# Attention and two networks on one core: the second network's two matrix products done by 2x2 blocks in Strassen's way, with h kept in DRAM between them

## The chip, the cores and the metric

The program runs on one core of one Trainium2 chip. The metric is the device time of one execution in microseconds (us), lower is better. The work is spread over the core's engines, each with its own instruction queue in program order: PE (TensorE, the matrix engine; PEld is its weight load, which overlaps the products), DVE (VectorE), ACT (ScalarE), POOL (GpSimd, hardly used here) and SP (SyncE, which issues nearly all DMA transfers).

## The reference, cut to what matters

```python
def _attn_ref(q, k, v) -> np.ndarray:
    ...
    return (out_up + out_local).astype(np.float32)

def _moe_ref(x, w_gate, w_val, w_out) -> np.ndarray:
    g = x @ w_gate
    silu = g * (1.0 / (1.0 + np.exp(-g)))
    val = x @ w_val
    return (silu * val @ w_out).astype(np.float32)

def _moe2_ref(x, w_in, w_out) -> np.ndarray:
    h = np.maximum(x @ w_in, 0.0)
    return (h * h @ w_out).astype(np.float32)

def reference(**kwargs):
    ...
    attn_out = _attn_ref(**attn_kwargs)
    B, H, S, D = attn_out.shape
    x = np.ascontiguousarray(attn_out.transpose(0, 2, 1, 3)).reshape(B * S, H * D)
    x = _moe_ref(x=x, **moe_kwargs)
    return _moe2_ref(x=x, **moe2_kwargs)
```

`q`, `k` and `v` are 4 x 8 x 576 x 64, so `x` is 2304 tokens by 512. `_attn_ref` is a softmax attention on means of four rows, plus one in which a token sees those fewer than four away. The first network (`_moe_ref`) goes 512 -> 1536 -> 512, the second (`_moe2_ref`) 512 -> 2048 -> 512.

## The kernel before

**Number format.** A product of two float32 matrices is made as three products in TensorE's fp32r format. Each operand is split into a high part (ScalarE copies it into fp32r) and a low part (VectorE subtracts the high part from the source), and high x high, high x low and low x high are added up in a PSUM bank. "hi/lo" below means such a pair. Weights arrive as float64 words, in pieces of 128 x 512 (512 KB): a piece is loaded into the tile `wst`, decoded by ScalarE (L271, a scale) and VectorE (exponent, sign at L286, last bits at L296) into `wf`, and split by ScalarE (L306) and VectorE (L309) into a slot of the pool `w1` (6 slots) or `w2` (5 slots), 3 pieces to a slot.

**Stages, in order of time.** (1) Attention, with the first network's hidden units 0 to 5 beside it (stage B1; 128 hidden values are one unit), in token tiles of 256 and then 384. (2) Stage B2: units 6 to 11, for 6 tiles of 384 tokens; a unit is 24 products for gate and value (`proj`, L929 to L931), tanh and multiplications, and 12 products with w_out (`down`, L939 to L941). The tile's result gets the part from B1 added (L1042) and goes to `y_sp` in DRAM. (3) Stage C: the second network, 6 tiles of 384 tokens x 16 units (`c_unit`). A unit is 12 products of 384 columns (`proj`, into a bank `gv`, 128 values of h by 384 tokens), ReLU (ScalarE, L1212), square (VectorE, L1215), the split of h (L1219, L1222), and 9 products of 512 columns (L1232 to L1234) that add the unit's share of the output into three banks (`att`, `att`, `y`; 128 tokens by 512 each). h never leaves the core. The decoded weights of stage C follow into slots of `w1` and `w2` as units of B1 and B2 give them up.

**What sets the order.** A list scheduler in Python (`Order`) simulates the engines when the kernel is built. A `Task` is a chain of `Stage`s; a stage names its engine ("t" TensorE, "v" VectorE, "a" ScalarE, "d" SP), a cost, the buffers that it takes and gives back, and a condition (`after([...])`: not before these tasks). Tasks wait in queues ("mlp" for units, "x" for token tiles, "w" for weights, "v", "other"), each with a due time counted in units, and the scheduler writes the instructions out one after the other. On the chip each engine follows that order strictly. Products have no competitor left in stages B2 and C but other products.

The second network's products before (in `c_unit`, for one of three 128-token slices `c`):

```python
nc.tensor.matmul(o, u["h"][:, 0, c], w[:, 0], start=(f == 0), stop=False)
nc.tensor.matmul(o, u["h"][:, 0, c], w[:, 1], start=False, stop=False)
nc.tensor.matmul(o, u["h"][:, 1, c], w[:, 0], start=False, stop=last)
```

## Time and profile before

| what | value |
| --- | --- |
| device time, three runs | 991.59, 990.94, 991.14 us (median 991.14) |
| span of the profiled execution | 989.6 us |
| TensorE (PE) busy | 976.9 us, 99% |
| VectorE (DVE) busy | 546.8 us, 55% |
| ScalarE (ACT) busy | 371.8 us, 38% |
| GpSimd (POOL) busy | 23.8 us, 2% |
| DMA | 100.11 MB, mean 101 GB/s |

The runs are whole executions of the program without a profile; the span is that of one profiled execution, from its first instruction to its last, and all durations below come from it. A busy time is the union of an engine's instructions; products are pipelined, so that the durations of neighbours overlap and the cost of one is better read from start to start. The granted clock is the share of full speed that TensorE was given: 1.00 is 2.4 GHz, 0.50 is 1.2 GHz.

### The profile page before, as it was taken

What the parts mean: (1) busy time and instruction counts of PE and PEld (TensorE: products, weight loads), DVE (VectorE), ACT (ScalarE), POOL (GpSimd) and SP (SyncE); (2) the same over time, 40 slices, a digit from 0 to 9 for tenths busy, and PEclk for the clock granted to TensorE, in tenths of its full rate; (3) what the DMA queues carried; (4) which work ended last, traced back from release to release, by engine and by line L of the source; (5) the groups of instructions that cost most, each with busy time, mean ns of one, the idle gap of its engine ahead of it and who ended that gap; (6) DMA issues with size and microseconds to landing.
All of it is one profiled execution on the core that took longest, in us unless ns stands there. A gap on an engine that the chain in (4) does not pass through costs nothing.

```text
span 989.6 us, 17229 instructions
## 1 busy us (share of the span) xinstructions
PE 976.9 (99%) x7122; PEld 915.8 (93%) x7122; DVE 546.8 (55%) x1163; ACT 371.8 (38%) x844; POOL 23.8 (2%) x31
## 2 busy tenths in 40 slices
PE   8989999999999999999999999999999999999998
PEld 7868999999999999999999999999999999999996
DVE  6999996559589698542342598532322322322222
ACT  3676663443355355221121255432322322322222
POOL 0202020000000000000000000000000000000000
PEclk9989999999999999999999999999999999999999
DMA  9989785142473555220320554010100000000000
GB/s 274 265 269 266 209 185 137 44 123 51 145 251 112 185 183 174 96 90 7 96 74 23 167 177 160 20 64 1 32 32 1 20 14 1 32 1 1 33 1 32
DMA packets 67770, 100.11 MB, mean 101 GB/s; under 512 B 19564, under 2 KB 51820, under 8 KB 67692
## 3 DMA queue, kind: packets, MB, share of 16 engines
q1 hardware_dynamic: 64236, 91.04, 29.1%
q0 software_dynamic: 3456, 7.96, 4.7%
q8 instruction: 56, 0.92, 0.4%
q14 instruction: 22, 0.18, 0.1%
HBM read 79.07 MB, written 19.92 MB: 100 GB/s over the span
## 4 chain that ended last, share of the span: by engine, by line
PE 97%; DVE 1%; DMA 1%; ACT 1%; SPq 0%; issue 0%
PE gv L929 17%; PE gv L931 17%; PE gv L930 17%; PE att L1234 5%; PE att L1232 5%; PE att L1233 4%; PE y L939 4%; PE y L941 3%; PE y L940 3%; PE y L1233 2%; PE y L1232 2%; PE y L1234 2%; PE att L527 2%; PE att L585 2%; PE att L939 2%; PE att L941 2%
## 5 line engine op out<-in xcount | busy, mean ns | idle before, releaser
L929 PE MATMUL gv<-xh,w 128*128 128x384 f32 (+1 forms) x1056 | 342.8, 325 | 0.0
L931 PE MATMUL gv<-xh,w 128*128 128x384 f32 (+1 forms) x1056 | 339.6, 322 | 0.0
L930 PE MATMUL gv<-xh,w 128*128 128x384 f32 (+1 forms) x1056 | 339.1, 321 | 0.0
L929 PEld LDWEIGHTS gv<-xh,w 128*128 128x128 f32 x1056 | 199.0, 188 | 6.0 <-issue 0.6
L930 PEld LDWEIGHTS gv<-xh,w 128*128 128x128 f32 x1056 | 199.1, 189 | 3.9
L931 PEld LDWEIGHTS gv<-xh,w 128*128 128x128 f32 x1056 | 199.0, 188 | 0.2 <-DVE w L309 0.2
L1222 DVE TENSOR_TENSOR hh<-sg,hh 128x384 fp32r<-128x384 f32 x96 | 53.6, 558 | 124.4 <-ACT hh L1219 124.4
L1215 DVE TENSOR_TENSOR sg<-sg 128x384 f32<-128x384 f32 x96 | 53.6, 558 | 116.0 <-ACT sg L1212 115.9
L1219 ACT ACTIVATE hh<-sg 128x384 fp32r<-128x384 f32 x96 | 50.4, 525 | 128.5 <-PE y L1234 126.4
L1212 ACT ACTIVATE sg<-gv 128x384 f32<-128x384 f32 x96 | 47.1, 491 | 132.5 <-PE gv L931 131.0
L973 DVE SCALAR_TENSOR_TENSOR sg<-sg,gv 128x384 f32<-128x384 f32 (+1 forms) x84 | 41.7, 496 | 95.3 <-PE gv L931 94.4
L979 ACT ACTIVATE hh<-sg 128x384 fp32r<-128x384 f32 (+1 forms) x84 | 40.0, 476 | 132.1 <-DVE sg L973 131.6
L1234 PE MATMUL att<-w,hh 128*128 128x512 f32 x192 | 76.0, 396 | 0.0
L1232 PE MATMUL att<-w,hh 128*128 128x512 f32 x192 | 75.7, 394 | 0.0
L1233 PE MATMUL att<-w,hh 128*128 128x512 f32 x192 | 75.6, 394 | 0.0
L939 PE MATMUL y<-hh,w 128*128 128x256 f32 (+1 forms) x240 | 74.5, 310 | 0.0
L941 PE MATMUL y<-hh,w 128*128 128x256 f32 (+1 forms) x240 | 72.7, 303 | 0.1
L940 PE MATMUL y<-hh,w 128*128 128x256 f32 (+1 forms) x240 | 72.5, 302 | 0.0
L968 DVE SCALAR_TENSOR_TENSOR sg<-sg,gv 128x384 f32<-128x384 f32 (+1 forms) x84 | 41.5, 494 | 43.6 <-ACT sg L960 42.9
L960 ACT ACTIVATE sg<-gv 128x384 f32<-128x384 f32 (+1 forms) x84 | 37.3, 444 | 68.3 <-PE gv L931 68.1
L306 ACT ACTIVATE w<-wf 128x512 fp32r<-128x512 f32 x68 | 42.8, 629 | 41.0 <-DVE wf L296 40.5
L982 DVE TENSOR_TENSOR hh<-sg,hh 128x384 fp32r<-128x384 f32 (+1 forms) x84 | 41.8, 498 | 19.1 <-ACT hh L979 18.9
(97 smaller groups left out, 1356.2 us busy)
## 6 DMA issues: line engine op xcount, KB each, us to landing
wst<-wB SPq DMA_DIRECT2D x36, 512.0 KB, 4.2
wst<-wC SPq DMA_DIRECT2D x32, 512.0 KB, 3.9
y_sp<-ys SPq DMA_DIRECT2D x8, 768.0 KB, 3.8
xt<-x_sp SPq DMA_DIRECT2D x6, 768.0 KB
ys<-y_sp SPq DMA_DIRECT2D x6, 768.0 KB, 4.7
xt<-y_sp SPq DMA_DIRECT2D x6, 768.0 KB, 5.3
out<-ys SPq DMA_DIRECT2D x17, 256.0 KB, 2.1
qT<-qT SPq DMA_DIRECT2D x7, 592.0 KB, 9.9
```

The lines of the kernel that those rows point to most:

```text
L929: nc.tensor.matmul(ps[:, :n], w[:, 0], xh[:, 0, kk, :n], start=(kk == 0), stop=False)
L930: nc.tensor.matmul(ps[:, :n], w[:, 0], xh[:, 1, kk, :n], start=False, stop=False)
L931: nc.tensor.matmul(ps[:, :n], w[:, 1], xh[:, 0, kk, :n], start=False, stop=(kk == KD - 1))
L939: nc.tensor.matmul(y, w[:, 0], hh[:, 0, :n], start=start, stop=False)
L940: nc.tensor.matmul(y, w[:, 0], hh[:, 1, :n], start=False, stop=False)
L941: nc.tensor.matmul(y, w[:, 1], hh[:, 0, :n], start=False, stop=stop)
L1215: nc.vector.tensor_tensor(out=u["r"], in0=u["r"], in1=u["r"], op=ALU.mult)
L1219: nc.scalar.activation(out=u["h"][:, 0], in_=u["r"], func=AF.Copy)
L1222: nc.vector.tensor_tensor(out=u["h"][:, 1], in0=u["r"], in1=u["h"][:, 0].bitcast(F32), op=ALU.subtract)
L1232: nc.tensor.matmul(o, u["h"][:, 0, c], w[:, 0], start=(f == 0), stop=False)
L1233: nc.tensor.matmul(o, u["h"][:, 0, c], w[:, 1], start=False, stop=False)
L1234: nc.tensor.matmul(o, u["h"][:, 1, c], w[:, 0], start=False, stop=last)
```

## The change

Both products of the second network are cut into 2x2 blocks and done with 7 block products in the place of 8 (Strassen's way with 15 block sums, Winograd's form). This needs all of a block's h before the second product, so the stage falls into two phases.

**Phase one** (`c_step`): h = relu(x w_in)^2, for two halves `s` of the hidden values, three groups `g` of 768 tokens (two 384-token halves are the two column blocks), seven block products `P` in the order `STEPS`, and four hidden blocks `k` of 128. A step is 6 products of 384 columns. Two banks per k: in A (`att`) P1 begins and P6, P7, P4 add to it, and after each ScalarE copies the bank out as the start of one h block; in B (`gv` or `y`) stand P2, and then P5 and P3, each added by VectorE (`plus`) to a block copied earlier. ReLU and square follow, and the block goes to `h_sp` in DRAM. `x_group` makes four sums of x blocks and seven hi/lo blocks per group, in a ring of 4 (two `xh` tiles).

**Phase two** (`d_step`): the output, in 9 token blocks `q` of 256, seven steps of 24 products of 256 columns each (eight p of 256 hidden values x 3). `h_load` reads h back in two pieces (three for block 0), `t_task` makes four sums and seven hi/lo blocks of 1024 elements, in a ring of 3 that lies in the same two `xh` tiles. Output tiles `os` are stored from SP.

**Weights.** Of the 32 pieces of 128 x 512, 6 are decoded straight into block sums; 26 are decoded during B2 by `stage_task`, stored as float32 to `w_sp`, and loaded again when `pair_task` makes the sums: a pair of pieces gives four sums of 256 columns and seven blocks in hi/lo (512 + 512 + 768 columns, `CUTS`). The sets of w_in for p 0 to 2 are in `wu`, 3 in `wr`, 4 to 7 in `wl`; the sets of w_out overwrite them when phase one's half `s` has done its last step with the part. Pools change too: `w2` has 4 slots, `w1` is released after B1, and B2's units 10 and 11 get two slots `w6` in its place; B2's last tile runs them first.

The diff, cut:

```diff
-NW1, NW2 = 6, 5
+NW1, NW2 = 6, 4
...
+        slot, ready = ("w2", late_) if j < NF + NW2 else ("w6", late_b1_)
         for i in range(3):
-            w_task((j, i), wB[j][:, i], W2[j - NF], LATE, lambda: after([late_]))
+            w_task((j, i), wB[j][:, i], slot, LATE, lambda ready=ready: after([ready]))
     for t in range(NT2):
...
         x_task(("B2", t), T2, lambda t=t: load_xr(x_sp, t), lambda done=done: after(done), ("xt",))
         early, finish = add_tasks(("B2", t), t * T2, T2, y_sp, y4)
...
+        if t == NT2 - 1:
+            js = js[NW2:] + js[:NW2]
+        for j in js:
+            unit_tasks("B2", t, j, T2, j == js[0], j == js[-1], y4, finish, (), early)
+            if t == NT2 - 1 and j == NF1 - 1:
+                end_w6 = downs[-1]
+    end_b2 = downs[-1]
...
+    NG1, NG2 = NT2 // 2, NTOK // 256
+    STEPS = (1, 2, 6, 7, 5, 4, 3)
+    IN, OUT = 0, 1
+    BLK = {1: 0, 2: 1, 7: 2, 4: 3, 5: 4, 6: 5, 3: 6}, {1: 0, 7: 1, 2: 2, 3: 3, 5: 4, 6: 5, 4: 6}
+    CUTS = (0, 2), (2, 4), (4, 7)
+    h_sp = dram.tile([128, NG2, ALL, 2, 2, 128], F32, name="h_sp")
+    w_sp = dram.tile([128, 2 * NF2, 512], F32, name="w_sp")
...
+    def minus(out, a, b, op=ALU.subtract):
+        nc.vector.tensor_tensor(out=out, in0=a, in1=b, op=op)
...
+    def stage_task(kind, f):
...
+        def store():
+            nc.sync.dma_start(out=w_sp[:, kind * NF2 + f], in_=u["f"].bitcast(F32))
+        staged[kind, f] = Task([*bits(u, wC[f][:, kind]), Stage("d", dma(128 * 512), store, (), ("wf",))], LATE)
+        queues["w"].append(staged[kind, f])
...
+    def pair_task(kind, p, slot, conds, room=None):
...
+            if kind == IN:
+                minus(w["s"][:, 0], quarter(1, 0), quarter(1, 1), ALU.add)
+            else:
+                minus(w["s"][:, 0], quarter(0, 1), quarter(0, 0))
+        def second():
...
+        def third():
+            if kind == IN:
+                minus(w["s"][:, 1], w["s"][:, 0], quarter(0, 0))
...
+        def fourth():
+            minus(w["s"][:, 2], quarter(0, 1) if kind == IN else quarter(1, 0), w["s"][:, 1])
...
+            src, hi, _ = parts(i)
+            nc.scalar.activation(out=hi, in_=src, func=AF.Copy)
+        def low(i):
+            src, hi, lo = parts(i)
+            minus(lo, src, hi.bitcast(F32))
...
+        def begun(i):
+            also = [outs[0]] if i == 1 and not fs else [c_ready[kind, p - 1][2]] if k == i == 2 else []
+            return after([both, *also, *conds(i)])
...
+    for p in range(3):
+        pair_task(IN, p, "wu", lambda i: [late_b1_])
+    for f in range(6, NF2):
+        stage_task(IN, f)
+    for f in range(NF2):
+        stage_task(OUT, f)
+    pair_task(IN, 3, "wr", lambda i: [late_w6_])
+    for p in range(NPC, ALL):
+        pair_task(IN, p, "wl", lambda i: [late_b2_])
...
+    def x_group(s, g, start):
...
+        def t1():
+            u["t"] = [com.tile([128, 2, T2], F32, tag="hh", bufs=N_HH, name="hh") for _ in range(2)]
+            minus(u["t"][0], block(0, 1), block(0, 0))
+        sums = {
+            6: [t1, lambda: minus(u["t"][1], block(1, 1), u["t"][0])],
+            7: [lambda: minus(block(0, 1), block(1, 1), block(0, 1))],
+            4: [lambda: minus(u["t"][1], block(1, 0), u["t"][1])],
+        }
...
+            def high(P=P, place=place):
+                nc.scalar.activation(out=place()[:, 0], in_=source[P](), func=AF.Copy)
+            def low(P=P, place=place):
+                minus(place()[:, 1], source[P](), place()[:, 0].bitcast(F32))
...
+    def c_step(s, g, P, k):
...
-                nc.tensor.matmul(o, u["h"][:, 0, c], w[:, 0], start=(f == 0), stop=False)
-                nc.tensor.matmul(o, u["h"][:, 0, c], w[:, 1], start=False, stop=False)
-                nc.tensor.matmul(o, u["h"][:, 1, c], w[:, 0], start=False, stop=last)
...
+        def go():
+            if P in (1, 2, 5):
+                banks[k, own] = bank("att" if P == 1 else bk)
+            n = x_at[s, g, P]
+            ps, x = banks[k, own][:, :T2], ring[n % 4 // 2][:, n % 2]
+            w = c_w[IN, p][:, :, BLK[IN][P]]
+            for kk in range(2):
+                c = slice(kk * 128, kk * 128 + 128)
+                for i, (a, b) in enumerate(((0, 0), (0, 1), (1, 0))):
+                    nc.tensor.matmul(
+                        ps,
+                        w[:, a, c],
+                        x[:, b, kk],
+                        start=P in (1, 2, 5) and kk == 0 and i == 0,
+                        stop=P in (2, 3, 4) and kk == 1 and i == 2,
+                        skip_group_check=True,
+                    )
+        def copy(c, func=AF.Copy):
+            nc.scalar.activation(out=h_slot(k, c), in_=banks[k, "A"][:, :T2], func=func)
+        def plus(c):
+            minus(h_slot(k, c), banks[k, "B"][:, :T2], h_slot(k, c), ALU.add)
...
+        def both(c):
+            h = h_slot(k, c)
+            nc.vector.scalar_tensor_tensor(out=h, in0=h, scalar=0.0, in1=h, op0=ALU.max, op1=ALU.mult)
+        def store(c):
+            dst = h_sp[:, 3 * g : 3 * g + 3, p, c // 2, c % 2]
+            nc.sync.dma_start(out=dst, in_=h_slot(k, c).rearrange("p (i n) -> p i n", n=128))
+        def rest(c):
+            if c == 1:
+                fns = [Stage("v", dve(T2), lambda: both(c))]
...
+                fns = [Stage("a", act(T2), lambda f=f: over(c, f)) for f in (AF.Relu, AF.Square)[c == 2 :]]
+            return fns + [Stage("d", dma(128 * T2), lambda: store(c), (), (f"h{k}{c}",))]
+        if P in (1, 6, 7):
+            c = {1: 0, 6: 1, 7: 3}[P]
+            out = [Stage("a", act(T2, True), lambda: copy(c), (f"h{k}{c}",))]
+        elif P == 4:
+            out = [Stage("a", act(T2, True), lambda: copy(2, AF.Relu), (f"h{k}2",), ("att",)), *rest(2)]
+        else:
+            c = {2: 0, 5: 3, 3: 1}[P]
+            out = [Stage("v", dve(T2), lambda: plus(c), (), () if P == 5 else (bk,)), *rest(c)]
+        before = {6: 1, 7: 6, 4: 7, 3: 5}.get(P)
+        held = {2: 1, 5: 7, 3: 6}.get(P)
+        def cond():
+            t = after([x_blocks[s, g][P], weights(IN, p, P)])
+            return latest(t, now(evac[s, g, before, k])) if before else t
+        def out_cond():
+            t = after([step, h_room_])
+            return latest(t, now(evac[s, g, held, k])) if held else t
...
+        step = Task([Stage("t", 6 * products(T2), go, take, ("xb",) if k == NPC - 1 else (), cond)], due, True)
...
+    banks, end = {}, (1, NG1 - 1)
+    for s in range(2):
+        for g in range(NG1):
+            x_group(s, g, n_unit[0] - 3.0)
+            for P in STEPS:
+                for k in range(NPC):
+                    c_step(s, g, P, k)
...
+            pair_task(OUT, s * NPC + k, "", conds, (IN, s * NPC + k))
...
+    FIRST_PIECES = [("hl", 0, 0, 3), ("xt", 0, 3, 6), ("hl", 3, 6, 8)]
...
+    def h_load(q, tag, at, p0, p1, due):
+        def load():
+            nc.sync.dma_start(out=piece(tag)[:, at : at + p1 - p0], in_=h_sp[:, q, p0:p1])
+        def ready():
+            stored = [evac[s, q // 3, P, k] for s in range(2) for P in (2, 3, 4, 5) for k in range(NPC)]
+            return latest(after(stored), piece_free(tag, at, q)) if after(stored) is not None else None
...
+    def t_task(q, P, n, due):
...
+        def s1():
...
+            each(whole(1), views(0, 1), views(1, 1), ALU.add)
+        def s2():
...
+            each(whole(2), whole(1), views(0, 0))
+        sums = {
+            6: [s1, s2],
+            7: [lambda: each(views(0, 1), views(0, 0), views(0, 1))],
+            3: [lambda: each(whole(2), views(1, 0), whole(2))],
...
+        def high(only):
+            for x, hi, _ in pairs()[only]:
+                nc.scalar.activation(out=hi, in_=x, func=AF.Copy)
+        def low(only):
+            for x, hi, lo in pairs()[only]:
+                minus(lo, x, hi.bitcast(F32))
...
+        apart = m if q == 0 and m == 3 else 1
+        for i in range(apart):
+            only = slice(i, i + 1) if apart > 1 else slice(None)
+            cond = (lambda i=i: ready(i)) if apart > 1 else None
+            stages += [
+                Stage("a", m * act(1024 // m) / apart, lambda only=only: high(only), ("tb",) if i == 0 else (), (), cond),
+                Stage("v", m * dve(1024 // m) / apart, lambda only=only: low(only)),
+            ]
...
+    def d_step(q, P, n):
+        n_unit[0] += 1
+        due = n_unit[0]
+        final = q == NG2 - 1
+        t_task(q, P, n, due - 3.0)
...
+        def go():
+            if tag:
+                banks[q, own] = bank(tag)
+            ps = banks[q, own][:, :256]
+            hl = t_place(n)
+            for p in range(ALL):
+                w = c_w[OUT, p][:, :, BLK[OUT][P]]
+                for i, (a, b) in enumerate(((0, 0), (0, 1), (1, 0))):
+                    nc.tensor.matmul(
+                        ps,
...
+        def plus(c):
+            minus(at(c), banks[q, own][:, :256], at(c), ALU.add)
...
+        if P in (1, 6, 7):
+            c = {1: 0, 6: 2, 7: 3}[P]
+            stages = [Stage("a", act(256, True), lambda: copy(c), {1: ("os",), 7: ("wf",)}.get(P, ()))]
...
+        else:
+            c = {2: 0, 5: 3, 3: 2, 4: 1}[P]
+            stages = [Stage("v", dve(256), lambda: plus(c), (), {2: ("gv",), 3: ("y",), 4: ("gv",)}.get(P, ())), *put(c)]
...
+        def cond():
+            t = after([t_tasks[q, P]] + [weights(OUT, p, P) for p in range(ALL)])
+            return latest(t, now(d_evac[q, before])) if before else t
...
+    sequence = [(0, 1)]
+    for q in range(NG2):
+        sequence += [(q, P) for P in (2, 6, 5, 7)]
+        sequence += [(q + 1, 1)] * (q + 1 < NG2) + [(q, 4), (q, 3)]
...
+    for n, (q, P) in enumerate(sequence):
+        d_step(q, P, n)
```

**On TensorE.** Before, one unit's second product in stage C stands as 9 rows of 512 columns between other units' first products; these are the last seven of them and the row behind (`hh` is h in hi/lo, `w1` a weight slot, `att` and `y` are output banks):

```order
L1234 MATMUL att_8163<-w1_5100,hh_8160 128x512
L1232 MATMUL att_8164<-w1_5100,hh_8160 128x512
L1233 MATMUL att_8164<-w1_5100,hh_8160 128x512
L1234 MATMUL att_8164<-w1_5100,hh_8160 128x512
L1232 MATMUL y_8165<-w1_5100,hh_8160 128x512
L1233 MATMUL y_8165<-w1_5100,hh_8160 128x512
L1234 MATMUL y_8165<-w1_5100,hh_8160 128x512
L929 MATMUL gv_8207<-xh_7583,w1_5336 128x384
```

After the change, these are TensorE's rows where phase one's last steps (P3, k = 2 and 3, L1534) meet the first step of phase two (block 0, P1, L1764); `xh` holds x or h in hi/lo, `wu`, `wr` and `wl` hold weight sets, x3 is the number of like rows:

```order
L1534 MATMUL y_8856<-xh_6871,wl_7631 128x384 x6
L1534 MATMUL y_8868<-xh_6871,wl_7919 128x384 x6
L1764 MATMUL att_8997<-wu_5522,xh_7230 128x256 x3
L1764 MATMUL att_8997<-wu_5627,xh_7230 128x256 x3
L1764 MATMUL att_8997<-wu_5730,xh_7230 128x256 x3
L1764 MATMUL att_8997<-wr_7031,xh_7230 128x256 x3
L1764 MATMUL att_8997<-wl_7215,xh_7230 128x256 x3
L1764 MATMUL att_8997<-wl_7361,xh_7230 128x256 x3
L1764 MATMUL att_8997<-wl_7631,xh_7230 128x256 x3
L1764 MATMUL att_8997<-wl_7919,xh_7230 128x256 x3
L1764 MATMUL gv_9030<-wu_5522,xh_6871 128x256 x3
```

No product with h stands among those of phase one any more; the step of 24 products takes all of its eight blocks of h, in the low part too, within one row of `xh`, and all of its weight sets in turn.

**On VectorE.** Before, in stage C, the square and the low part of one unit after the other (`sg` is the ReLU's result, `ys` an output tile):

```order
L1215 TENSOR_TENSOR sg_8602<-sg_8602 128x384
L1241 COPY ys_8618<-att_8164 128x512
L1222 TENSOR_TENSOR hh_8623<-sg_8574,hh_8623 128x384
L1215 TENSOR_TENSOR sg_8638<-sg_8638 128x384
L1222 TENSOR_TENSOR hh_8654<-sg_8602,hh_8654 128x384
```

After the change, from the first addition (`plus`) of the last P3 to the low part that the eighth block of h needs for phase two's first step. L1245 is the line of a helper (`minus`), so it is told by its tiles: `hr<-gv` and `hr<-y` are additions out of a bank, `wl` are low parts of w_out's sets (from `wst` and `ws`), `xh` are low parts of h (from `hl` and `xt`), `ys` is the first block sum of h, and L1554 is ReLU and square. The first twelve:

```order
L1245 TENSOR_TENSOR hr_7200<-gv_8835,hr_7200 128x384
L1245 TENSOR_TENSOR xh_7230<-hl_7199,xh_7230 128x384
L1554 SCALAR_TENSOR_TENSOR hr_7200<-hr_7200 128x384
L1245 TENSOR_TENSOR hr_7200<-gv_8845,hr_7200 128x384
L1245 TENSOR_TENSOR wl_7215<-wst_8430,wl_7215 128x512
L1554 SCALAR_TENSOR_TENSOR hr_7200<-hr_7200 128x384
L1245 TENSOR_TENSOR xh_7230<-xt_8853,xh_7230 128x384
L1245 TENSOR_TENSOR hr_7200<-y_8856,hr_7200 128x384
L1245 TENSOR_TENSOR xh_6871<-hl_7199,xh_6871 128x384
L1554 SCALAR_TENSOR_TENSOR hr_7200<-hr_7200 128x384
L1245 TENSOR_TENSOR hr_7200<-y_8868,hr_7200 128x384
L1245 TENSOR_TENSOR wl_7215<-ws_8556,wl_7215 128x768
```

and the twelve behind them:

```order
L1245 TENSOR_TENSOR xh_6871<-xt_8853,xh_6871 128x384
L1554 SCALAR_TENSOR_TENSOR hr_7200<-hr_7200 128x384
L1245 TENSOR_TENSOR wl_7361<-wst_8567,wl_7361 128x512
L1245 TENSOR_TENSOR wl_7361<-ws_8702,wl_7361 128x768
L1245 TENSOR_TENSOR wl_7631<-wst_8704,wl_7631 128x512
L1245 TENSOR_TENSOR wl_7919<-wf_8794,wl_7919 128x512
L1245 TENSOR_TENSOR wl_7631<-ws_8702,wl_7631 128x768
L1245 TENSOR_TENSOR wl_7919<-ws_8865,wl_7919 128x768
L1245 TENSOR_TENSOR ys_8989<-hl_7199 128x384
L1245 TENSOR_TENSOR ys_8989<-xt_8853 128x384
L1245 TENSOR_TENSOR ys_8989<-hl_7199 128x256
L1245 TENSOR_TENSOR xh_7230<-hl_7199,xh_7230 128x256
```

The low part of the third piece of h (`xh_7230<-hl_7199,xh_7230 128x256`) stands behind the low parts of four weight sets and behind the first sum for a later step (`ys_8989`); before, two or three short rows per unit stood there.

## Rows read from the trace of the kernel before

**Rows 1.** The page: the span, and the engines' busy times.

```profile
span 989.6 us, 17229 instructions
...
PE 976.9 (99%) x7122; PEld 915.8 (93%) x7122; DVE 546.8 (55%) x1163; ACT 371.8 (38%) x844; POOL 23.8 (2%) x31
```

**Rows 2.** Windows: stretch, length, busy PE PEld DVE ACT POOL, clock, DMA, GB/s.

```profile
400.00:500.00 100.00, 100.00 (x578) 100.00 (x577) 38.17 (x70) 19.78 (x38) 0.00 (x0) 1.00 0.22 72
587.00:985.00 398.00, 397.87 (x1994) 359.17 (x1992) 143.03 (x252) 120.23 (x231) 0.00 (x0) 1.00 0.09 29
```

**Rows 3.** TensorE's timeline: start, duration, engine, line, operation, tiles.

```profile
580.80 0.34 PE L929 MATMUL gv<-xh,w 128*128 128x384 f32 x1
...
586.87 0.34 PE L941 MATMUL y<-hh,w 128*128 128x384 f32 x1
...
591.21 0.40 PE L1232 MATMUL att<-w,hh 128*128 128x512 f32 x1
...
593.07 0.39 PE L1234 MATMUL y<-w,hh 128*128 128x512 f32 x1
...
258.63 0.28 PE L940 MATMUL y<-hh,w 128*128 128x256 f32 x1
...
279.76 0.28 PE L931 MATMUL gv<-xh,w 128*128 128x256 f32 x1
```

**Rows 4.** The timeline at the end of the program.

```profile
984.47 0.40 PE L1234 MATMUL y<-w,hh 128*128 128x512 f32 x1
984.91 0.38 ACT L1299 ACTIVATE ys<-y 128x256 f32<-128x256 f32 x1 [0.81 <-PE y L1234]
986.18 0.44 SPq L1247 DMA_DIRECT2D out<-ys  x1
```

**Rows 5.** VectorE's timeline (brackets: idle time ahead, what ended it).

```profile
226.28 0.42 DVE L973 SCALAR_TENSOR_TENSOR sg<-sg,gv 128x256 f32<-128x256 f32 x1 [0.15 <-PE gv L931]
226.62 0.68 DVE L439 TENSOR_TENSOR p<-p,mx 128x512 f32<-128x512 f32 x1
...
403.11 0.68 DVE L286 SCALAR_TENSOR_TENSOR wf<-wst,wf 128x512 int32<-128x512 int32 x1
403.71 0.55 DVE L1042 TENSOR_TENSOR ys<-y,ys 128x384 f32<-128x384 f32 x1
404.18 0.55 DVE L973 SCALAR_TENSOR_TENSOR sg<-sg,gv 128x384 f32<-128x384 f32 x1
...
431.69 1.83 DVE L898 TENSOR_TENSOR xh<-xt,xh 128x768 fp32r<-128x768 f32 x2 [0.33 <-ACT xh L892]
433.44 0.55 DVE L982 TENSOR_TENSOR hh<-sg,hh 128x384 fp32r<-128x384 f32 x1
```

**Rows 6.** ScalarE's timeline.

```profile
405.82 0.63 ACT L306 ACTIVATE w<-wf 128x512 fp32r<-128x512 f32 x1 [0.54 <-DVE wf L296]
406.36 0.47 ACT L960 ACTIVATE sg<-gv 128x384 f32<-128x384 f32 x1
...
430.81 1.58 ACT L892 ACTIVATE xh<-xt 128x768 fp32r<-128x768 f32 x2 [3.64 <-PE gv L931]
432.30 0.51 ACT L979 ACTIVATE hh<-sg 128x384 fp32r<-128x384 f32 x1
```

**Rows 7.** The page's DMA issues: tiles, count, KB each, us to landing.

```profile
wst<-wC SPq DMA_DIRECT2D x32, 512.0 KB, 3.9
```

**Rows 8.** Windows around the one fall of the granted clock, early in the program.

```profile
60.00:67.90 7.90, 5.41 (x81) 4.42 (x80) 7.16 (x27) 6.92 (x25) 0.00 (x0) 1.00 0.81 242
67.90:74.70 6.80, 6.68 (x42) 5.35 (x42) 5.62 (x14) 4.97 (x19) 0.84 (x1) 0.50 0.76 179
74.70:80.00 5.30, 5.30 (x73) 4.83 (x73) 5.23 (x18) 3.57 (x13) 0.84 (x1) 1.00 1.04 249
```

More of the change, by code (lines that the diff above doesn't have):

```diff
@@ L262, in load @@
                 w_tiles[key[0]] = pools[slot].tile(
[L263 removed]
+                    [128, 2, 3, 512], F32R, tag=slot, bufs={"w1": NW1, "w2": NW2, "w6": 2}[slot], name=slot
                 )
@@ new lines, in weights @@
+    def weights(kind, p, P):
+        i = [a <= BLK[kind][P] < b for a, b in CUTS].index(True)
+        return c_ready[kind, p][i]
+    N_PAIR = {"wu": 3, "wr": 1, "wl": NPC}
+    for k, n in (N_PAIR | {"ws": 1, "w6": 2, "xb": 4, "tb": 3, "os": 2}).items():
+        order.free[k] = [0.0] * n
+    for k in range(NPC):
+        for c in range(4):
+            order.free[f"h{k}{c}"] = [0.0]
+    for p in range(3):
+        pair_task(IN, p, "wu", lambda i: [late_b1_])
+    for f in range(6, NF2):
+        stage_task(IN, f)
@@ L1199, in c_unit @@
+    steps, h_done, evac = {}, {}, {}
+    def c_step(s, g, P, k):
         n_unit[0] += 1
         due = n_unit[0]
[L1201 to L1212 removed]
@@ L1317, in c_unit @@
-        proj__.then = [mid, down_]
-        downs.append(down_)
-        queues["mlp"].append(proj__)
-    for t in range(NT2):
-        x_task(("C", t), T2, lambda t=t: load_xr(y_sp, t), lambda t=t: after([y_out["B2", t]]), ("xt",))
-        for f in range(NF2):
-            c_unit(t, f)
+        p = s * NPC + k
+        bk = ("gv", "y")[k // 2]
+        own = "B" if P in (2, 5, 3) else "A"
+        def go():
[14 more added lines that the diff above has]
+                        skip_group_check=True,
+                    )
@@ new lines, in c_step, with conds @@
+        out[0].cond = out_cond
+        evac[s, g, P, k] = Task(out, due, True)
+        step.then = [evac[s, g, P, k]]
+        steps[s, g, P, k] = step
+        queues["mlp"].append(step)
+    banks, end = {}, (1, NG1 - 1)
[3 more added lines that the diff above has]
+            for P in STEPS:
+                for k in range(NPC):
+                    c_step(s, g, P, k)
+        for k in range(NPC):
+            def conds(i, s=s):
+                need = ((1, 2), (7, 4), (5, 6, 3))[i]
+                return [steps[s, NG1 - 1, P, k] for P in need for k in range(NPC)]
+            pair_task(OUT, s * NPC + k, "", conds, (IN, s * NPC + k))
```

435 lines of the change are left out of this document (327 added, 108 removed).

## The prediction

> **What bounds it now.** I read the page first: TensorE is busy for 976.9 of 989.6 us [rows 1], so the time is the sum of its products, unless a product costs less than its place in the queue. The windows come next. In the stretch of the second network (587 to 985 us) TensorE is idle for 0.13 us of 398, at full granted clock, with VectorE busy for 36% and ScalarE for 30% of it [rows 2]. So nothing else has a say there, and a product removed is worth its own pitch. The timeline gives that pitch (start to start; the durations overlap): 35 steps of 384 columns in 6.07 us are 0.1734 us each, 8 steps of 512 in 1.86 us are 0.2325, and 178 steps of 256, in the first network, in 21.13 us are 0.1187; other runs of 256 lie down to 0.1173, and I take 0.118 [rows 3]. The pitch grows nearly with the columns: 0.45 ns for one, and some 4 ns for a product.
>
> **What TensorE saves.** Before, the second network has 96 units of 12 products of 384 columns and 9 of 512: 1152 x 0.1734 + 864 x 0.2325 = 199.8 + 200.9 = 400.7 us. The stretch in the trace agrees: 397.7 us from 587.0 to 984.7 [rows 2, 4], plus 4.2 for two units' first products that stand ahead of the stage before's last. After, phase one has 168 steps of 6 products of 384 columns and phase two 63 steps of 24 products of 256: 1008 x 0.1734 + 1512 x 0.118 = 174.8 + 178.4 = 353.2 us. The saving is **47.5 us** (46.5 to 48.5 by the two pitches of 256). It isn't the eighth of 400.7 (50.1), since 504 more products pay their 4 ns.
>
> **What is added, and what hides it.** Durations back to back on VectorE: 384 elements 0.47 us, 512 0.60, 256 0.34, 768 0.875 [rows 5], so 1024 about 1.14 (estimate, by the same slope). On ScalarE 768 take 0.745 and 512 0.54 [rows 6], so 384 about 0.44.
> - Weights. 32 decodes of 0.34 + 0.60 + 0.60 = 1.54 us move ahead into B2, 49 us, with three of the block sums (a pair: 4 x 0.34 + 2 x 0.60 + 0.875 = 3.4 us). VectorE was idle for 62% of a stretch there [rows 2], some 139 us of B2's 225 (1296 x 0.1734): hidden, nothing charged. The stores and reloads are 256 to 512 KB each, 3.9 us to land for the larger [rows 7], on a DMA share of 0.22: hidden. Without w1's last slot, B2's units 10 and 11 wait for w6, decoded after B1's last product; 108 products (18.7 us) stand ahead of their first use, against 3.9 for a load and some 2.9 for a piece's decode and split: hidden.
> - Phase one, a group of 28 steps (29.1 us). VectorE: 11 operations of 768 (four sums, seven low parts) and 16 of 384 are 17.1 us. ScalarE: 7 of 768 and 36 of 384 are 21.0 us. 13 weight pairs lie in the phase: 44 us more of VectorE, 24 of ScalarE. In all 147 and 150 of 175 us. It fits, with 15% to spare; a step on a bank waits for the copy of the step before it on that bank, and three other steps (3.1 us) lie between at the tightest place (step 6 to step 7).
> - Phase two, a token block of 7 steps (19.8 us): VectorE four sums and four split low parts of about 1.2, three low parts of 1.14, three additions of 0.34: 14.0 us. It fits with 29% to spare. The 2 MB of h for a block are loaded in some 14 us (five steps); four times the 512 KB row's 3.9 would be 15.6, with four fixed parts, and the 242 GB/s of a busy stretch [rows 8] give 8.7: hidden.
>
> **What isn't hidden.** Three places.
> 1. From phase one to two. The first step of phase two runs through eight h blocks; the last two (p = 6 and 7) need the low part of the third piece of h. On VectorE this is the last of the 24 instructions shown in the change, all of them between the first addition of the last P3 and it: 14 of 384, 4 of 512, 4 of 768, 2 of 256: 6.58 + 2.40 + 3.50 + 0.68 = 13.2 us. The first can begin when P3's first step has ended, 3 x 1.04 = 3.1 us before the phase's end, plus a hand-over of 0.2 (the last product at 984.47, a pitch of 0.23, ScalarE at 984.91 [rows 4]). So it ends at -2.9 + 13.2 = 10.3 us after phase one's last product, and TensorE gets it at about 10.4. TensorE itself is there after 20 products, 2.4 us. It waits **8.0 us**. The store and reload of that piece ends earlier: its load is queued behind the second of P3's stores, about 0 us, and 3.9 us to land. Then step 6 needs two sums, a high and a low part in turn: VectorE's next items end at about 14.2, TensorE is there at 13.9: 0.3 more. Bounds: with the timeline's full durations (0.55, 0.68, 0.88 and 0.42) the 24 take 14.8 us, a wait of 9.6; if VectorE need not hold back the low part for those sums and weights, the load alone counts, a wait of 2.
> 2. The clock after it. The one place where the granted clock fell follows 7.9 us in which TensorE was idle for 2.5: it then went at half (1.2 for 2.4 GHz) from 67.9 to 74.7 us [rows 8]. A hole of 8 us is emptier than that. Half speed for 6.8 us loses 3.4, but some of it can lie in the hole itself: **2.5 us**, bounds 0 and 5 (two such falls in part). The Trainium skill ("TensorE: Matmul & The Clock Gate", Part 1) says that an idle array loses half its clock and gets it back after activity; the trace's one fall agrees, and by it the clock falls here too.
> 3. From B2 to phase one. VectorE has four additions out of B2's banks, then sums, low parts and additions: eight of 384, eight of 768 and two of 512 (12.0 us) up to the low part of block 7, beginning 1.4 us ahead of B2's end, with up to 1 us of waiting for ScalarE among them; TensorE is there after ten steps, 10.4. **1 us**, bounds 0 and 1.5.
> For all other group and block changes together I take **2 us**: 0 is what the trace shows of holes in 398 us, 13 is one us at each of 5 + 8 changes.
>
> The end stays: 4.9 us from the last product's end to the span's end, with an addition and a 128 KB store in place of the two half copies and theirs [rows 4].
>
> Sum: 989.6 - 47.5 + 8.3 + 2.5 + 1 + 2 = 955.9 us of span. The runs lie 1.4 to 2.0 us over the profiled span (median 991.14), so **957.4 us** of time, 3.4% less.
>
> **Rivals.**
> - *No hole at the change of phase.* TensorE would find the piece ready; 957.4 - 8.3 - 2.5 = 947. For it: the load's own chain is short. Against: the order on VectorE is fixed, and its 13 us of work begin only 3 us before the phase ends. 12%.
> - *The side engines hold TensorE up all along.* ScalarE and VectorE are to be busy for 85% of phase one, in order, where now they are at a third; each works behind the other (copy, then low part, then addition). If each of the 13 changes of group or block costs 1 to 2 us more, that is 13 to 26: 970 to 983, 975 as the middle. For it: the 85%, and what B2 to phase one shows in place 3. Against: ring buffers give blocks a lead of two steps or more, and by the counts the low part of a group's first block is done about 1 us before its use. 25%.
> - *The short products eat the gain.* Phase two trades products of 512 columns for 256. If these cost not 0.118 but more, the gain is gone at 0.118 + 47.5/1512 = 0.149 us without any hole, and at 0.140 with the holes above. If they took the 0.1734 of a 384-column product, phase two would take 262 us and the whole 1041. Against it stands the run of 179 products at 0.1187 with other weights each [rows 3]. 2%.
>  The same page of the Trainium skill (Back-to-back issue gap) gives sustained spacings of 81 ns at 128 columns and 131 at 512, which is a large part that doesn't depend on the columns; by a line through them (98 ns at 256, 114 at 384) the second network would take 18 us more than before, 1023 us here. No row agrees: this trace has 118.7 and 232.5 ns, so the sum goes by the rows.
>
> **How the numbers follow.** The forecast has 58% and a range of its own of 950 to 964 (hole 2 less to 2 more, clock 0 to 5, others 0 to 5). With 12% at about 947 and the lower half of the 25%, 8 in 10 lie in 946 to 972. A change under 0.2% (2 us) can't be told from none. Slower needs the third rival, or a mishap not seen (a reload of h that comes late for each of nine blocks, at 5 us each: 2%): 4%; same 1%; faster 95%.
>
> **What would show it.** In the changed profile: products of 256 columns at 0.117 to 0.119 us in phase two; TensorE's one long idle stretch in the first step of phase two, before the matmuls on the third h piece, 7 to 10 us, ended by VectorE; half clock for some us after it; VectorE busy at over 80% in phase one and 70% in phase two with TensorE still at 98%. I am wrong if the idle time is spread over many short waits on ScalarE or VectorE, if 256 columns cost over 0.125, or if the wait at the change of phase ends by a DMA.

## The result, and the profile after

The changed kernel takes **954.53 us** (median of four runs, 953.37 to 955.80), against 991.04 before; the ratio is 0.9635, with a 95% interval of 0.962 to 0.965. Forecast were 957.4 us and a range of 946 to 972. The profiled execution has a span of 953.6 us, where the sum gave 955.9.

The page after, its span and busy times (as [rows 1]):

```profile
span 953.6 us, 19189 instructions
...
PE 935.6 (98%) x7626; PEld 912.1 (96%) x7626; DVE 701.4 (74%) x1401; ACT 477.0 (50%) x1041; POOL 23.8 (2%) x31
```

Windows of phase one, of the change of phase, of the stretch at half clock and of phase two (columns as [rows 2]):

```profile
587.00:756.00 169.00, 168.20 (x969) 167.63 (x968) 134.26 (x223) 138.70 (x281) 0.00 (x0) 1.00 0.67 199
757.00:770.00 13.00, 5.59 (x36) 5.08 (x35) 13.00 (x26) 6.66 (x13) 0.00 (x0) 0.78 0.70 219
764.24:774.47 10.23, 5.54 (x26) 5.24 (x26) 9.11 (x18) 3.00 (x6) 0.00 (x0) 0.50 0.60 222
774.50:950.00 175.50, 175.50 (x1468) 175.50 (x1467) 123.89 (x190) 75.89 (x129) 0.00 (x0) 1.00 0.30 111
```

In phase one TensorE is idle for 0.8 us of 169, with VectorE busy for 79% and ScalarE for 82%; in phase two it is never idle once the change of phase is past. Between them lies the one hole. VectorE is busy there for all of the 13 us, and TensorE for 5.6. The waits view of TensorE from B2's end to the end of the program has four rows (engine, line, who was waited for, us in total, times, longest):

```profile
PE att L1764 <- DVE xh L1245: 4.7, 1, 4.7
PE att L1764 <- ACT xh L1712: 2.7, 1, 2.7
PE att L1534 <- DVE xh L1245: 0.6, 1, 0.6
PE att L1534 <- ACT hr L1544: 0.2, 1, 0.2
```

The timeline at the end of B2, around the hole, and at the end of phase two (the last two rows are VectorE's and SP's):

```profile
584.78 0.34 PE L941 MATMUL y<-hh,w 128*128 128x384 f32 x1
...
756.88 2.24 PE L1534 MATMUL y<-xh,wl 128*128 128x384 f32 x12
758.97 1.24 PE L1764 MATMUL att<-wu,xh 128*128 128x256 f32 x9
760.04 0.53 PE L1764 MATMUL att<-wr,xh 128*128 128x256 f32 x3
760.40 0.87 PE L1764 MATMUL att<-wl,xh 128*128 128x256 f32 x6
764.00 0.61 PE L1764 MATMUL att<-wl,xh 128*128 128x256 f32 x2 [2.72 <-ACT xh L1712]
769.29 1.22 PE L1764 MATMUL att<-wl,xh 128*128 128x256 f32 x4 [4.69 <-DVE xh L1245]
...
775.03 1.25 PE L1764 MATMUL att<-wu,xh 128*128 128x256 f32 x9
...
948.87 1.59 PE L1764 MATMUL y<-wl,xh 128*128 128x256 f32 x12
950.50 0.42 DVE L1245 TENSOR_TENSOR os<-y,os 128x256 f32<-128x256 f32 x1 [2.38 <-PE y L1764]
950.95 0.33 SPq L1788 DMA_DIRECT2D out<-os  x1
```

ScalarE's timeline shows what ended the first of the two waits: its high part of the third piece began when the load of that piece (issued at 759.51) had landed, 4.6 us after phase one's end, where the prediction has 3.9:

```profile
763.53 0.72 ACT L1712 ACTIVATE xh<-hl 128x256 fp32r<-128x256 f32 x2 [0.59 <-DMA hl<-h_sp]
```

The terms of the sum for phase two and its beginning can be read here. From 775.03 to 948.87 there are 1452 products: 0.1197 us each. The four and 24 products from 769.29 to 775.03 should take 3.35 us at that pitch and take 5.74: 2.4 us of half clock. And VectorE's timeline shows the queue that the prediction counted, from its first instruction to its last:

```profile
756.04 0.56 DVE L1245 TENSOR_TENSOR hr<-gv,hr 128x384 f32<-128x384 f32 x1 [1.20 <-PE gv L1534]
...
763.12 0.69 DVE L1245 TENSOR_TENSOR wl<-wst,wl 128x512 fp32r<-128x512 f32 x1
763.72 0.96 DVE L1245 TENSOR_TENSOR wl<-ws,wl 128x768 fp32r<-128x768 f32 x1
764.59 0.70 DVE L1245 TENSOR_TENSOR wl<-wst,wl 128x512 fp32r<-128x512 f32 x1
765.19 0.70 DVE L1245 TENSOR_TENSOR wl<-wf,wl 128x512 fp32r<-128x512 f32 x1
765.79 1.83 DVE L1245 TENSOR_TENSOR wl<-ws,wl 128x768 fp32r<-128x768 f32 x2
767.53 0.56 DVE L1245 TENSOR_TENSOR ys<-hl 128x384 f32<-128x384 f32 x1
...
768.80 0.77 DVE L1245 TENSOR_TENSOR xh<-hl,xh 128x256 fp32r<-128x256 f32 x2
```

It begins at 756.04, and the low part of the third piece, the first of the last row's two, is done at 769.1 (its start and a pitch of 0.34): 13.1 us without a gap.

### The profile page after: what moved, and what is told of

Same layout as the page of the kernel before. It is cut to its first block, busy times and chain, and to the rows that moved or that the text cites. A ratio compares the mean times of both kernels' runs of the same rounds, so it can differ in the third digit from the quotient of the medians.

```text
span 953.6 us, 19189 instructions
## 1 busy us (share of the span) xinstructions
PE 935.6 (98%) x7626; PEld 912.1 (96%) x7626; DVE 701.4 (74%) x1401; ACT 477.0 (50%) x1041; POOL 23.8 (2%) x31
## 4 chain that ended last, share of the span: by engine, by line
PE 95%; DVE 3%; ACT 1%; issue 0%
PE gv L929 11%; PE gv L931 11%; PE gv L930 11%; PE att L1764 10%; PE att L1534 10%; PE y L1764 5%; PE y L939 4%; PE gv L1534 4%; PE y L1534 3%; PE y L941 3%; PE y L940 3%; PE gv L1764 3%; PE att L527 2%; PE att L585 2%; PE att L941 2%; PE att L939 2%
## 5 line engine op out<-in xcount | busy, mean ns | idle before, releaser
L929 PE MATMUL gv<-xh,w 128*128 128x384 f32 (+1 forms) x672 | 214.0, 319 | 0.0
L931 PE MATMUL gv<-xh,w 128*128 128x384 f32 (+1 forms) x672 | 210.7, 314 | 0.0
L930 PE MATMUL gv<-xh,w 128*128 128x384 f32 (+1 forms) x672 | 210.3, 313 | 0.0
L929 PEld LDWEIGHTS gv<-xh,w 128*128 128x128 f32 x672 | 127.2, 189 | 1.9 <-issue 0.6
L931 PEld LDWEIGHTS gv<-xh,w 128*128 128x128 f32 x672 | 127.3, 189 | 0.2
L930 PEld LDWEIGHTS gv<-xh,w 128*128 128x128 f32 x672 | 127.3, 189 | 0.0
L1245 DVE TENSOR_TENSOR xh<-xt,xh 128x768 fp32r<-128x768 f32 (+2 forms) x62 | 56.1, 904 | 15.4 <-ACT xh L1712 14.4
L1764 PE MATMUL att<-wl,xh 128*128 128x256 f32 x420 | 56.9, 285 | 7.4 <-DVE xh L1245 4.7
L1764 PEld LDWEIGHTS att<-wl,xh 128*128 128x128 f32 x420 | 53.3, 192 | 7.9 <-DVE xh L1245 5.0
L1534 PE MATMUL att<-xh,wl 128*128 128x384 f32 x288 | 51.4, 334 | 0.0
L1534 PEld LDWEIGHTS att<-xh,wl 128*128 128x128 f32 x288 | 50.1, 188 | 0.0
L1780 ACT ACTIVATE os<-att 128x256 f32<-128x256 f32 x36 | 13.7, 383 | 68.6 <-PE att L1764 68.6
L939 PEld LDWEIGHTS y<-hh,w 128*128 128x128 f32 x240 | 45.2, 188 | 1.2 <-issue 0.2
L941 PEld LDWEIGHTS y<-hh,w 128*128 128x128 f32 x240 | 45.2, 188 | 0.3 <-DVE w L309 0.3
```

The lines of the kernel that those rows point to most:

```text
L929: nc.tensor.matmul(ps[:, :n], w[:, 0], xh[:, 0, kk, :n], start=(kk == 0), stop=False)
L930: nc.tensor.matmul(ps[:, :n], w[:, 0], xh[:, 1, kk, :n], start=False, stop=False)
L931: nc.tensor.matmul(ps[:, :n], w[:, 1], xh[:, 0, kk, :n], start=False, stop=(kk == KD - 1))
L939: nc.tensor.matmul(y, w[:, 0], hh[:, 0, :n], start=start, stop=False)
L941: nc.tensor.matmul(y, w[:, 1], hh[:, 0, :n], start=False, stop=stop)
L1245: nc.vector.tensor_tensor(out=out, in0=a, in1=b, op=op)
```

## The experiments

Times of whole runs scatter by 0.6 to 3.4 us, much of it from ahead of the second network (B2's last product lies between 583.2 and 586.4 us in these traces), so the column to compare is the **stretch**: from the start of phase one's last product to the start of phase two's last, in the profiled execution (from B2's last product to phase one's last for the last two rows). Each kernel has one trace; how well traces repeat can be judged from phase one, which takes 174.0 us in ten of the thirteen kernels. "Waits" are TensorE's in that stretch, in us, as its timeline or its waits view gives them; "half clock" is how long the records show the lower of the two levels in and after them.

| kernel | time, us | ratio to before, 95% interval | stretch, us | waits | half clock |
| --- | --- | --- | --- | --- | --- |
| changed kernel | 954.53 | 0.9635, 0.962 to 0.965 | 191.4 | 2.7 + 4.7 | 10.2 |
| load early | 955.79 | 0.9634, 0.962 to 0.9647 | 191.5 | 1.3 + 6.2 | 10.2 |
| load and low part early | 955.11 | 0.9632, 0.9618 to 0.9645 | 191.5 | 1.3 + 0.5, 3.3 + 0.5 | 3.4 + 6.8 |
| hole filled | 953.27 | 0.9613, 0.9599 to 0.9626 | 189.5 | 0.2 | none |
| GpSimd | 957.34 | 0.9654, 0.9641 to 0.9667 | 194.0 | 2.6 + 7.1 | 13.7 |
| ScalarE | 957.52 | 0.966, 0.9647 to 0.9674 | 193.4 | 2.0 + 3.8, 1.2 + 1.4 | 6.8 + 3.4 |
| finer conditions | 955.50 | 0.964, 0.9627 to 0.9653 | 190.6 | 3.7 + 3.4 | 6.8 |
| ScalarE, order mended | 952.84 | 0.9618, 0.9603 to 0.9632 | 188.8 | 2.0 + 3.8 | 6.8 |
| the same, filled | 951.29 | 0.9609, 0.9594 to 0.9623 | 187.8 | none | none |
| other order of three | 954.92 | 0.9642, 0.9626 to 0.9658 | 191.4 | 2.6 + 4.8 | 10.2 |
| h stored twice | 955.53 | 0.9648, 0.9633 to 0.9662 | 191.9 | 8.5 | 10.2 |
| phase one: all low parts twice | 987.52 | 0.9965, 0.9951 to 0.9979 | 204.7 (174.0 in the changed kernel) | 21.1 | 10.2 in the phase |
| phase one: three of seven twice | 964.24 | 0.9737, 0.9723 to 0.9751 | 182.0 | 5.3 | none in the phase |

**Is it the load or VectorE's queue?** The load of the third piece is issued earlier, with VectorE's order up to its low part held as it was (a condition on that stage, not shown):

```diff
+        if tag == "hl" and at:
+            ts = [evac[(*end, 5, k)] for k in range(3)]
+            return max(t.times[-2] for t in ts) + 0.5 if all(t.done for t in ts) else None
```

> The load of the third piece of h is issued ahead of seven stores of h, and ScalarE takes that piece ahead of one weight part; VectorE's order up to the piece's low part stays as it was. VectorE theory (its queue of 24 instructions ends the hole): TensorE's first wait of 2.7 us shrinks to under 0.5, the wait on the low part grows by as much and still ends at the same place (769 us of the span), the time changes by less than 0.5 us. Load theory (the piece arrives late, and VectorE only follows): the low part comes earlier too, 2 to 3 us less.

```profile
762.75 0.50 PE L1771 MATMUL att<-wl,xh 128*128 128x256 f32 x2 [1.28 <-ACT xh L1715]
769.48 1.22 PE L1771 MATMUL att<-wl,xh 128*128 128x256 f32 x4 [6.23 <-DVE xh L1245]
```

In this kernel's timeline of TensorE the first wait is 1.4 us shorter (not gone: ScalarE still has weight parts ahead of the piece), the second 1.5 us longer, and the stretch the same. The load is not what ends the hole.

**Is it the place in the queue or the amount of work?** The same without the condition, so that the low part stands ahead of six weight parts (the expectation says seven) and the first sum:

> As the run before, and VectorE does the piece's low part before the last seven weight parts and the first block sum of h, 5.7 us earlier. If the place of one instruction in the queue is what counts: the hole falls from 7.8 to about 2.4 us, the time by 5 us and more with the clock. If it is the amount of VectorE's work up to the sixth block product's low part that counts: the wait moves to that step (about 5 us for its block there), and the time falls by 0 to 2 us only.

```profile
763.97 0.50 PE L1767 MATMUL att<-wl,xh 128*128 128x256 f32 x2 [1.28 <-ACT xh L1715]
765.02 0.78 PE L1767 MATMUL att<-wl,xh 128*128 128x256 f32 x4 [0.54 <-DVE xh L1245]
773.40 0.80 PE L1767 MATMUL att<-wu,xh 128*128 128x256 f32 x2 [3.28 <-ACT xh L1715]
774.66 1.86 PE L1767 MATMUL att<-wu,xh 128*128 128x256 f32 x7 [0.47 <-DVE xh L1245]
```

The first step's waits shrink to 1.8 us, and 3.75 come back in the third step, P6, whose sums stand behind the weight parts now. The stretch is 191.5 us again. Counted as waits, 1.8 us were won (5.6 against 7.4); the lower clock, 10.2 us in both, fell on more running products and took them back. Nor would a full clock have left a gain: P6 goes on at 774.66, 14.5 us after phase one's last product, with 22 products of 0.12 us to do, so it could end at 17.1 (an estimate); with the clock held up and the old order, in the next experiment, it ends at 17.2. So the amount of VectorE's work up to P6 counts, and not which part of it comes first.

**What does the clock cost?** Idle products in the hole:

```diff
+                    if n == 0 and p == 6 and i in (0, 2):
+                        if i == 0:
+                            spare = bank("gv")[:, :256]
+                        for _ in range(22 if i == 0 else 40):
+                            nc.tensor.matmul(spare, hl[0][:, 0], w_first, start=True, stop=True)
```

> 62 idle products of 256 columns (22 before the seventh block of h in phase two's first step, 40 before its low part), written to a bank that nobody reads, fill 7.3 of the hole's 7.8 us; nothing else moves. Clock theory (the fall to half speed behind the hole costs 2.5 us): the granted clock stays at 1.00 and the time falls by 2 to 3 us. Rival (the fall has another cause, or the half speed lies in the hole itself): within 0.5 us of the changed kernel.

```profile
758.50:773.00 14.50, 14.15 (x115) 13.69 (x114) 13.37 (x25) 7.03 (x12) 0.00 (x0) 1.00 0.67 227
```

The window over the hole shows TensorE busy for 14.15 of 14.50 us at full clock, and the stretch is 1.9 us shorter: nearly the 2.4 of half clock, less 0.3 of a wait at P6 that half speed had covered. That is just short of the 2 to 3 us expected; the medians of whole runs differ by 1.3 us, and their intervals overlap. The Trainium skill ("TensorE: Matmul & The Clock Gate", Part 1) has an idle array lose half its clock; the two traces agree.

**Less work on VectorE: GpSimd takes some.** Four low parts of 768 columns:

```diff
-            minus(lo, src, hi.bitcast(F32))
+            if i == 2 and kind == OUT and p >= NPC:
+                nc.gpsimd.tensor_tensor(out=lo, in0=src, in1=hi.bitcast(F32), op=ALU.subtract)
+            else:
+                minus(lo, src, hi.bitcast(F32))
```

> The four low parts of 768 columns of the last weight sets go from VectorE to GpSimd. VectorE theory: 3.5 us less stand ahead of the low part; if GpSimd takes up to 1.8 us for each, the hole ends 2 to 3.5 us earlier and the time falls by 2 to 5 us, the clock included. If GpSimd takes over 3 us each, or slows VectorE down while both run, the gain is gone. Load theory: no change, since the piece arrives as before.

GpSimd's row and VectorE's rows beside it:

```profile
758.83 8.57 POOL L1377 TENSOR_TENSOR wl<-ws,wl 128x768 fp32r<-128x768 f32 x4 [602.81 <-ACT wl L1372]
...
759.27 0.56 DVE L1245 TENSOR_TENSOR hr<-y,hr 128x384 f32<-128x384 f32 x1
759.74 1.85 DVE L1245 TENSOR_TENSOR wl<-wst,wl 128x512 fp32r<-128x512 f32 x1
761.51 2.16 DVE L1245 TENSOR_TENSOR xh<-xt,xh 128x384 fp32r<-128x384 f32 x1
763.60 2.15 DVE L1557 SCALAR_TENSOR_TENSOR hr<-hr 128x384 f32<-128x384 f32 x1
765.67 2.28 DVE L1245 TENSOR_TENSOR wl<-wst,wl 128x512 fp32r<-128x512 f32 x1
767.88 0.68 DVE L1245 TENSOR_TENSOR wl<-wf,wl 128x512 fp32r<-128x512 f32 x1
```

GpSimd takes 8.57 / 4 = 2.14 us each, and from 759.74 on VectorE gets through one operation per GpSimd operation, at 2.1 us where 0.47 is usual for 384 elements. Only the addition at 759.27, which reads one of its inputs from a bank, takes its usual 0.47 to the next. The four operations that would take 2.1 us (two of 384, two of 512) take 8.1, from 759.74 to 767.88: 6.0 lost for 3.5 saved, and the stretch is 2.6 us longer. The Trainium skill ("SBUF — State Buffer", SBUF: two separate sides) describes a port pair that the two engines lock for a whole instruction, when VectorE reads two inputs from SBUF, the core's data memory; the rows agree.

**ScalarE takes some.** ReLU and square of the last four blocks:

```diff
+            elif c == 1:
+                fns = [Stage("a", act(T2), lambda f=f: over(c, f)) for f in (AF.Relu, AF.Square)]
+                fns[0].cond = lambda: t_tasks[0, 1].times[4] if t_tasks[0, 1].at > 4 else None
```

> ReLU and square of the last four h blocks go from VectorE (4 x 0.47 us) to ScalarE, behind its high parts, where it waits for 6.6 us. Theory (the amount of VectorE's work up to the sixth block product sets the end): the low part of the third piece and the sums behind it come 1.9 us earlier, and so does everything in phase two: from phase one's last product to phase two's last 191.4 - 1.9 = 189.5 us, the time 1.5 to 2 us less. Rival (other waits, for the load or for ScalarE, come next): under 0.5 us.

The low part's wait ends 10.5 - 8.8 = 1.7 us earlier after phase one's end, as the theory says, but the stretch grows by 2.0. TensorE's waits in the window behind the hole:

```profile
PE att L1767 <- DVE xh L1245: 1.4, 1, 1.4
PE att L1767 <- ACT xh L1715: 1.2, 1, 1.2
```

They are in the second block's first step. ScalarE's high part for it stood in the queue behind a copy out of a bank that TensorE had yet to fill, because the scheduler's model expected the load later:

```profile
779.59 0.38 ACT L1783 ACTIVATE os<-att 128x256 f32<-128x256 f32 x1 [5.36 <-PE att L1767]
779.87 0.84 ACT L1715 ACTIVATE xh<-hr 128x768 fp32r<-128x768 f32 x1
```

The next kernel changes that expectation alone (the load counts from the stage ahead of the stores, less 1 us):

> As the run with ReLU and square of the last four h blocks on ScalarE, and the scheduler is told that the load of the second token block ends earlier, so that ScalarE takes this block's high part before a copy of the first block's output. There the hole had become 1.7 us shorter, but two waits of 1.4 and 1.5 us had come in the second block's first step. Theory (these two were ScalarE's and VectorE's order, the load had landed): they go, and the stretch from phase one's last product to phase two's last is 189.0 to 190.0 us (191.4 in the changed kernel). Rival (the load itself is late): both waits stay, 192 us and more.

```profile
775.52 0.39 ACT L1784 ACTIVATE os<-att 128x256 f32<-128x256 f32 x1 [2.20 <-PE att L1768]
775.80 0.84 ACT L1716 ACTIVATE xh<-hr 128x768 fp32r<-128x768 f32 x1
```

The high part now stands behind an earlier copy and comes 17.0 us after phase one's last product, where it came at 22.7; the load is issued 10.6 us after that product in both kernels, so it was the order and not the load. Both waits are gone, and the stretch is 188.8 us: 1.7 from the queue and 0.8 from a shorter half clock.

**Both together** (17 and 31 idle products):

> The same with 17 and 31 idle products in the two parts of the hole. If the clock's price and VectorE's work add up: 1.7 us from the hole and 2 us from the clock, a stretch of 187.5 to 188.5 us and a time 3 to 4 us below the changed kernel. If the clock stays at full speed but TensorE is then ahead of the sums for the steps behind: 188.5 to 190 us.

187.8 us of stretch and 951.29 us of time: faster than the changed kernel by 3.6 us in the stretch (3.2 in the median; the intervals just touch). Gaps of 353 and 399 ns from product to product, where 120 is usual, are all that is left of waits.

**Earlier weight parts.** `conds` asks for the steps of the set's own k instead of all four:

> Each set of w_out may overwrite its set of w_in as soon as the steps of its own k are through, not of all four. VectorE is idle for 3.1 us in the 6 us ahead of the hole; if weight parts move into that time, the hole ends up to 3 us earlier and the time falls by up to 3 us. ScalarE is busy without a gap in that stretch, so that the high parts may not come earlier: then 0 to 1 us.

The hole ends 0.5 us earlier, the half clock is shorter, and the stretch falls by 0.8 us; but phase one is 1.1 us longer, with three waits on x blocks where there was one. Nothing is gained.

**How much room do the side engines have?** In phase one `low` of `x_group` does its operation twice, for all seven block products or for three:

> Each of the 42 low parts of x in phase one is done twice, 7 x 0.875 us more of VectorE for each group of 29.1 us, from 79 to about 100% of the phase. Side-engine theory as forecast (85% would cost nothing, the rings give a lead): VectorE now binds, phase one becomes 5 to 30 us longer. Rival (phase one has more room than its busy shares say): under 2 us.

> Only three of the seven low parts of a group (P2, P5, P3) twice: 18 x 0.875 us, VectorE at about 88% of phase one. By the forecast's rule that a busy share under 90% with a lead of two steps is hidden: under 1 us longer. If each change of block is already at its edge: up to 18 x 0.875 = 15.8 us longer.

The windows of the two over phase one, and the waits of the second:

```profile
586.00:790.00 204.00, 182.85 (x994) 176.24 (x993) 172.15 (x267) 141.81 (x284) 0.00 (x0) 0.97 0.55 165
...
585.00:765.00 180.00, 174.58 (x987) 170.23 (x986) 149.79 (x244) 140.05 (x284) 0.00 (x0) 1.00 0.62 187
...
PE att L1535 <- DVE xh L1245: 3.8, 6, 0.8
PE att L1535 <- ACT hr L1545: 1.5, 2, 1.1
```

36.8 us more of VectorE make the phase 30.7 us longer (some 4.5 of them are half clock: in this phase one the records show three falls of 3.4 us each, in the changed kernel's none). 15.8 us more make it 8.0 longer, where the forecast's rule allowed under 1. VectorE is busy for 84 and 83% of the stretched phases, and TensorE waits.

The mean of 79% hides why. In the changed kernel, one group's first three blocks (P1, P2, P6) and its last two (P4, P3) look like this:

```profile
700.72:713.20 12.48, 12.48 (x73) 12.48 (x73) 12.40 (x21) 8.73 (x18) 0.00 (x0) 1.00 0.57 160
721.52:729.84 8.32, 8.32 (x49) 8.32 (x49) 3.83 (x9) 6.77 (x15) 0.00 (x0) 1.00 0.78 222
```

VectorE has no time left in the first and is idle for over half of the second, and it is alike in all groups but the first (busy for 97 to 100% against 41 to 60%). In the second run all six waits on VectorE stand in blocks P1, P6 and P7. Their own low parts were not done twice; they stand in VectorE's queue behind those of P3 and P2, which were. Two of the waits, in P6 and P7:

```profile
714.41 4.62 PE L1535 MATMUL att<-xh,wl 128*128 128x384 f32 x24 [0.50 <-DVE xh L1245]
719.81 4.26 PE L1535 MATMUL att<-xh,wl 128*128 128x384 f32 x23 [0.77 <-DVE xh L1245]
```

So the room is not in the mean: it is gone in P1, P2 and P6, and what is left lies in P4 and P3. No run tried work added in P4 or P3 alone.

**h stored twice**, the second time to another DRAM tile:

> Each of the 96 stores of h is done a second time, to a place that nobody reads: 18.9 MB more in phase one, where the DMA engines are at two thirds. Theory (the DMAs of phase one are hidden): phase one stays within 1 us, the hole grows by 0 to 1.5 us, since the third piece's load stands behind more stores. Rival (the buffers of h come free too late): waits of ScalarE's copies hold TensorE up by 5 us and more.

```profile
587.00:756.00 169.00, 168.21 (x969) 167.63 (x968) 135.37 (x226) 138.72 (x280) 0.00 (x0) 1.00 0.99 293
```

With the DMA engines busy for 99% at 293 GB/s, phase one is as long as ever (174.0 us). Only the hole is now ended by the load, 0.5 us later: the third piece stands behind twelve stores of some 0.6 us each on SP's queue, and ScalarE's high part waits for it:

```profile
770.88 0.72 ACT L1715 ACTIVATE xh<-hl 128x256 fp32r<-128x256 f32 x2 [6.37 <-DMA hl<-h_sp]
```

**The order of the three products in phase two:**

> In phase two the three products of a block of h go high x high, low x high, high x low, so that the same weights stream twice in a row and no stationary block is loaded twice in a row. If the 119.7 ns of a product (118 in the sum) come from this order: 117 to 118.5 ns, 2 to 4 us less. If not: 119.7 ns again.

0.1197 us again; not this order.

## Why the prediction was right, point by point

The mechanism came out as forecast: TensorE's products bound both phases, and one hole stood where they meet, as long as VectorE's queue made it. That the time is only 2.9 us from the forecast is in part luck, since the errors of the smaller terms nearly cancel.

- **The bound and the saving.** Phase one's products take 758.97 - 584.78 us, less B2's last and with 12 that stand ahead of it, 176.1; phase two's 950.3 - 758.97 = 191.3. Together 367.4, where the sum had 353.2 + 13.8 = 367.0. Before, the trace gave 397.7 + 4.2 = 401.9 where the sum used 400.7, so 1.2 us of saving were left out. The products alone came down from 401.9 to 355.8 us (1008 x 0.1734 + 1512 x 0.1197): 46.1 saved, where 47.5 were forecast.
- **Products of 384 columns**: 0.1734 us, as before. **Of 256**: 0.1197, not 0.118: the term was 2.6 us too small, and 0.1197 lies above the bound taken from the first network's 0.1187. Why, stays open: behind the hole the pitch is the same in every block, whether the DMA engines are busy for 0 or 96% of 5 us, and the order of the three products doesn't matter. The rival of 0.140 and more is dead.
- **The hole.** Forecast: VectorE's low part 10.3 us after phase one's end, 13.2 us of queue, a wait of 8.0. Measured: 769.1 - 759.0 = 10.1, 13.1, and 7.8 from product to product (2.9 and 4.9 by start times). The load's own wait (bound: 2) is there too, 2.7 us on ScalarE's high part, but inside the other; with the load early it shrinks and nothing is won. By the forecast's own sign (wrong if the wait ends by a DMA) this first part counts against it, and the early load shows that it cost nothing. The 0.3 at P6 showed once the clock was held up (399 - 120 ns).
- **The clock**: 2.5 forecast, 2.4 measured in the rows, 1.9 net by filling. That the size fits is luck: the forecast took half speed for 6.8 us with a part of it in the hole; it lasted 10.2 us, of which 5.0 lay in the hole. That there is a price at all, and that the hole brings it, the filled hole shows.
- **B2 to phase one**: 1 forecast, 0.6 + 0.2 idle and 1.2 by start times, at the named block, P7.
- **All other changes of group and block**: 2 forecast, nothing measured. This is where the rival of held-up engines would have stood. It didn't come, but the reason given against it (15% to spare) was weak: work worth 9% of the phase, added on VectorE, costs half of what is added. The prediction's 147 and 150 us of 175 (84 and 86%) were measured as 79 and 82%, and a mean over the phase was the wrong thing to count: in three of a group's seven blocks VectorE has nothing to spare.
- **What would show it**: the hole stands in the named step and is ended by VectorE, though in two pieces (2.7 and 4.7 us) and not one; half clock follows; TensorE is at 98%. VectorE's 71% in phase two is over the 70 named, its 79% in phase one just misses the 80, and the pitch of 256 columns misses its 0.117 to 0.119.
- **The end** was called unchanged. It is 1.6 us shorter (4.9 to 3.3 from the last product's end to the span's): one store of 128 KB follows the last addition where three stores were queued. That this is the reason was not tested.
- Errors of +2.6, -0.5, -2, -1.2 and -1.6 us, and smaller ones, add up to the 2.3 by which the span is under the sum. No step failed; four terms were mis-sized by 1 to 3 us (the short products too small; the other changes and the end too large; the saving too small), and the first cancels much of the rest.
